# Second to fourth token block transposed by VectorE strips and a trip through DRAM instead of by TensorE

## The chip, the cores and the metric

The kernel runs on one core of a Trainium2 chip. The metric is the device time of one execution in microseconds (us); lower is better. The core has a matrix engine (TensorE, PE in the profile), VectorE (DVE), ScalarE (ACT), GpSimd (POOL) and SyncE (SP), which issues most of the transfers. All tensors are float32.

## What is computed

One layer on 2048 tokens of width 448: a layer norm, then attention with a compressive memory and a gated feed-forward network side by side, both added to the input. The reference, cut:

```
xn = layernorm(x)                                  # 2048 x 448
q, k, v = xn @ wq, xn @ wk, xn @ wv                # 16 heads of 28
for s in range(4):                                 # blocks of 512 tokens
    p = softmax(q_s k_s^T * scale + causal mask)
    a_mem = phi(q_s) M / (phi(q_s) z)              # memory of the earlier blocks
    o_s = g * a_mem + (1 - g) * p v_s
    M += phi(k_s)^T v_s;  z += sum phi(k_s)
A = o @ wo
B = (sigmoid(xn @ w_gate) * (xn @ w_up)) @ w_down  # 448 -> 1792 -> 448
out = x + A + B
```

## The kernel before

The program has a front (four blocks of 512 tokens, one after the other) and a long later part, in which the feed-forward network, the attention and the output projection share the engines.

A block of the front needs the normalised tokens with the 448 features on the partitions: `xs[b]`, a tile of 128 x 7 x 512. The features are in chunks of 128, 128, 128 and 64; the first 64 are kept twice in chunk 3. Each product is made in three parts, high by high, high by low and low by high, so `xs[b][:, 0:4]` holds the values rounded to the matrix engine's type and `xs[b][:, 4:7]` (and rows 64 to 127 of chunk 3) the differences to the full value. `TERMS` lists the eleven matmuls of a product: chunk 0 high by high, high by low, low by high, and so on.

In block b the order on TensorE is: four times `values` (11 matmuls into `pv`, one group of 128 tokens each; with a read of the memory, `recall`, behind some of them from the third block on), then seven times `keys_queries` (11 matmuls into `pp`, one chunk of 128 key or query features, k counts them), with `key_rows` (four transposes into `pk`) behind k = 2 to 5 and `update` (64 small matmuls into `pmm`) behind k = 6. Between them stands the preparation of block b+1: `statistics`, `rstd`, and for each of four token groups `normalise` (VectorE, L346) and `turn`, which is four TensorE transposes into a bank `pt` (L103), one ScalarE copy to the high part (L105) and two VectorE differences for the low part (L110, L111). `keys_queries` has ScalarE copy the product (L382), for keys and late queries two more passes there (L386, L387), a VectorE difference (L388), a store to DRAM (`qd`, L389) and a VectorE pass for `e` (L391).

On TensorE, ScalarE and VectorE the instructions of the front stand in the order in which the code writes them; the queues of SP and GpSimd are ordered by a scheduler. Each SP transfer also waits until the transfer eight before it has landed. `acc[b]` (128 x 4 x 448) holds the input of block b: the norm reads it, and later the products of both branches are added to it (L183, L831). `x_block(b)` loads it with token t*128 + p on partition p.

Of the kernel before, what the change touches and what calls it, by code (L numbers as in the profile page):

```python
# [9 lines left out]
F32 = mybir.dt.float32  # L10
# [59 lines left out]
def kernel(  # L70
# [45 lines left out]
    def x_block(b):  # L116
        return x[b * L:(b + 1) * L, :].rearrange("(t p) d -> p t d", p=P)

    ps = ctx.enter_context(tc.tile_pool(name="psum", bufs=1, space=PSUM))

# [27 lines left out]
    fd = [dram.tile([D, L], F32, name=f"fd{b}") for b in range(NB)]  # L148
    vd = [dram.tile([P, NT, H * 32], F32, name=f"vd{b}") for b in range(NB)]
    od = [dram.tile([H * 32, L], F32, name=f"od{b}") for b in range(NB)]  # L150

# [22 lines left out]
    def gated():  # L174
# [21 lines left out]
        def load_down(f, tag="rawd"):  # L196
            raw_down[f] = (mid.tile([P, 1024], F32, name="raw", bufs=2)[:, :D] if tag == "raw" else
                           mid.tile([P, D], F32, name="rawd", bufs=1))
            nc.sync.dma_start(raw_down[f], w_ffn[f][:, 1024:])
# [24 lines left out]
        for f0 in range(0, NF, FG):  # L224
# [3 lines left out]
            if f0 == 0:  # L228
                ahead[0, 0] = lambda: (load_down(1, "raw"), ready_up(1))
                ahead[0, 2] = lambda: load_up(2)  # L230
                ahead[1, 3] = lambda: load_up(3)
# [70 lines left out]
    with tc.tile_pool(name="front", bufs=2) as sb, tc.manual_schedule(engines=FRONT):  # L302
# [41 lines left out]
        def normalise(b, t, mean, y):  # L344
            xn = sb.tile([P, 512], F32, name="xn")
            V.tensor_scalar(xn[:, :D].rearrange("p (m h c) -> p h m c", h=H, c=4),  # L346
                              acc[b][:, t, :].rearrange("p (h m c) -> p h m c", h=H, c=4), mean, y,
                              op0=ALU.subtract, op1=ALU.mult)
            if b == 0:
                A.activation(xn[:, D:], xn[:, 384:D], AF.Copy)  # L350
            else:
                G.tensor_copy(xn[:, D:], xn[:, 384:D])
            return xn

        def turn(b, t, xn):
            transpose_split(bank("pt", "s"), xn, xs[b], t)

# [15 lines left out]

        stored = {}

# [74 lines left out]
        for c in range(4, 6):  # L450
            raw_qk.append(two_k("wqk_raw"))
            nc.sync.dma_start(raw_qk[c], w_qk[c])
        nc.sync.dma_start(acc[1], x_block(1))
        raw_qk.append(four_k(F32, "wqk_raw")[:, 0, :])
# [77 lines left out]
        for b in range(NB):  # L532
            last = b == NB - 1
            phi, xn = {}, {}
            if b > 1:
# [16 lines left out]
            if st and b > 0:  # L552
                st = rstd(*st)
                for n in range(2):
                    xn[n] = normalise(b + 1, n, *st[n])
            e = {}
            for k, c in enumerate((3, 4, 5, 6, 0, 1, 2) if last else range(7)):
# [13 lines left out]
                if (b, k) in ((0, 3), (1, 0)):  # L571
                    with tc.issue_after(stored[b, c]):
                        nc.sync.dma_start(acc[b + 2], x_block(b + 2))
                if (b, k) in ((2, 1), (3, 0)):
                    with tc.issue_after(stored[b, c]):
                        next(ffn)
                if last:
                    if k > 0:
                        next(ffn)
                    if 2 <= k < 6:  # L580
                        phi[k - 2] = phi_queries(b, k - 2)
                    if k > 4:
                        begin[k - 5]()
                        recall(b, k - 5, phi[k - 5])
                    continue
                if 2 <= k < 6:
                    key_rows(k - 2, e[k - 2])
                if k == 6:
                    update(b)
                n = k - 1 if b == 0 else k + 1  # L590
                if 2 <= n < 6:
                    turn(b + 1, n - 2, xn[n - 2])
                if 0 <= n < 4 and n not in xn:
                    xn[n] = normalise(b + 1, n, *st[n])
                if b == 2 and k == 6:
# [295 lines left out]
```

## Time and profile before

| | us |
|---|---|
| median of 3 runs (lowest to highest) | 680.28 (679.64 to 680.9) |
| the profiled execution | 679.62 |
| its span | 677.8 |
| TensorE busy in the span | 671.3 |
| VectorE busy | 569.2 |
| ScalarE busy | 338.6 |
| GpSimd busy | 149.3 |

The span is the time from the first to the last instruction of the profiled execution; the rest of its time lies around it. Rows of the profile name the source line (L103), the engine, the operation, the tile that is written and those that are read, the count, the busy time and the mean length of one in ns. A chain row has its start, its length and the work. The clock granted to TensorE was 0.999 over the span.

### The profile page before, as it was taken

How to read it: one execution, taken by the hardware profiler on the slowest of the kernel's cores; microseconds unless marked ns; L12 is line 12 of the kernel's file. 1: busy time of each engine (PE TensorE's matmuls, PEld its weight loads, DVE VectorE, ACT ScalarE, POOL GpSimd, SP SyncE). 2: the span in 40 equal slices, each digit the busy share in tenths (PEclk: the TensorE clock that was granted, in tenths of full speed). 3: DMA queues.
4: the chain of work that ended last, by engine and by line, in shares of the span. 5: the costliest groups of instructions: out<-in, count | busy, mean ns of one | idle time of the engine just before them, and what ended most of it. 6: DMA issues, size and time to landing. Idle time of an engine off the chain costs nothing.

```text
span 677.8 us, 11106 instructions
## 1 busy us (share of the span) xinstructions
PE 671.3 (99%) x3882; PEld 558.9 (82%) x3882; DVE 569.2 (84%) x987; ACT 338.6 (50%) x563; POOL 149.3 (22%) x360
## 2 busy tenths in 40 slices
PE   8999999999999999999999999999999999999998
PEld 7888888778878788788877878788787887888897
DVE  6765786685889899989989889899998899999854
ACT  4847564434454555555545455465545554544320
POOL 4520111001222222132222213232122221321000
PEclk9999999999999999999999999999999999999999
DMA  7446676794423133232325432325342432423352
GB/s 271 175 165 248 214 266 219 291 312 125 113 71 101 58 103 101 54 115 88 70 59 130 103 82 57 102 57 129 81 106 57 98 78 70 107 78 79 84 172 102
DMA packets 46327, 84.59 MB, mean 125 GB/s; under 512 B 6552, under 2 KB 20928, under 8 KB 45760
## 3 DMA queue, kind: packets, MB, share of 16 engines
q1 hardware_dynamic: 42736, 76.26, 36.9%
q0 software_dynamic: 3392, 7.52, 5.0%
q8 instruction: 31, 0.51, 0.3%
q14 instruction: 24, 0.20, 0.1%
q10 hardware_dynamic: 144, 0.11, 0.0%
HBM read 51.05 MB, written 32.64 MB: 123 GB/s over the span
## 4 chain that ended last, share of the span: by engine, by line
PE 97%; DMA 1%; DVE 1%; SPq 0%; ACT 0%; issue 0%; DVEq 0%
PE pgu L255 42%; PE pd L181 20%; PE pp L381 10%; PE st L639 6%; PE pa L725 5%; PE po L824 5%; PE pv L361 5%; PE n L433 2%; DMA acc<-in_x 1%; PE pt L103 1%; PE pk L401 1%; PE pmm L412 1%; DVE stats L320 0%; DVE xn L346 0%; DVE xs L110 0%
## 5 line engine op out<-in xcount | busy, mean ns | idle before, releaser
L255 PE MATMUL pgu<-xs,wgu 128*128 128x512 f32 x1232 | 302.6, 393 | 0.0
L255 PEld LDWEIGHTS pgu<-xs,wgu 128*128 128x128 f32 x1232 | 228.9, 188 | 46.4 <-issue 2.0
L181 PE MATMUL pd<-wdn,hh 128*128 128x448 f32 x672 | 155.3, 366 | 0.0
L181 PEld LDWEIGHTS pd<-wdn,hh 128*128 128x128 f32 x672 | 122.7, 188 | 11.6 <-issue 0.8
L654 POOL TENSOR_SCALAR_AFFINE_SELECT w<-w 128x256 f32<-128x256 f32 (+1 forms) x160 | 76.1, 478 | 231.5 <-ACT w L643 162.5
L707 ACT ACTIVATE w<-w 128x1024 f32<-128x1024 f32 (+1 forms) x96 | 87.9, 915 | 57.9 <-DVE w L703 57.9
L643 ACT ACTIVATE w<-st 128x512 f32<-128x512 f32 x128 | 75.6, 592 | 62.3 <-PE st L639 57.8
L703 DVE TENSOR_TENSOR w<-w,mb 128x1024 f32<-128x1024 f32 (+1 forms) x96 | 100.6, 1055 | 0.8
L661 DVE TRANSPOSE_TENSOR_REDUCE mx<-w 128x32 f32<-128x1024 f32 x64 | 78.9, 1233 | 6.6 <-POOL w L654 6.5
L381 PE MATMUL pp<-xs,wqk 128*128 128x512 f32 x308 | 77.7, 401 | 0.0
L183 DVE TENSOR_TENSOR acc<-pd,acc 128x448 f32<-128x448 f32 x112 | 67.5, 602 | 6.3 <-PE pd L181 6.3
L278 ACT ACTIVATE hh<-sg 128x512 fp32r<-128x512 f32 x56 | 35.3, 631 | 67.1 <-DVE sg L272 42.8
L381 PEld LDWEIGHTS pp<-xs,wqk 128*128 128x128 f32 x308 | 56.8, 188 | 13.4 <-issue 2.4
L639 PE MATMUL st<-qk 84*128 84x128 f32 (+3 forms) x256 | 62.1, 314 | 0.1
L262 ACT ACTIVATE sg<-pgu 128x512 f32<-128x512 f32 x56 | 33.2, 593 | 50.3 <-PE pgu L255 50.3
L639 PEld LDWEIGHTS st<-qk 84*128 84x128 f32 x256 | 47.9, 189 | 9.0 <-issue 1.4
L272 DVE SCALAR_TENSOR_TENSOR sg<-sg,pgu 128x512 f32<-128x512 f32 x56 | 37.7, 673 | 10.9 <-PE pgu L255 10.9
L388 DVE TENSOR_TENSOR qk<-pp,qk 128x512 fp32r<-128x512 f32 x28 | 19.3, 688 | 27.5 <-ACT e L386 21.5
L689 DVE STREAM_TRANSPOSE mb<-top 128x1024 f32<-128x1024 f32 x32 | 39.5, 1235 | 3.3 <-POOL top L686 3.2
L361 PE MATMUL pv<-wv,xs 128*128 128x448 f32 x176 | 39.8, 377 | 0.2
L281 DVE SCALAR_TENSOR_TENSOR hh<-sg,hh 128x512 fp32r<-128x512 f32 x56 | 38.3, 684 | 0.9 <-DMA qk<-qd 0.7
L725 PE MATMUL pa<-w,vv 128*32 128x128 f32 (+3 forms) x512 | 37.8, 436 | 0.0
(98 smaller groups left out, 624.4 us busy)
## 6 DMA issues: line engine op xcount, KB each, us to landing
qk<-qd SPq DMA_DIRECT2D x192, 112.0 KB
qd<-qk SPq DMA_DIRECT2D x28, 512.0 KB
raw<-in_w_ffn SPq DMA_DIRECT2D x14, 512.0 KB
vd<-vst SPq DMA_DIRECT2D x4, 1024.0 KB
vv<-vd SPq DMA_DIRECT2D x16, 256.0 KB
od<-w POOLq DMA_DIRECT2D x16, 256.0 KB, 4.2
sums<-od SPq DMA_DIRECT2D x32, 128.0 KB
out<-acc SPq DMA_DIRECT2D x15, 224.0 KB
```

What stands on the lines that cost most here:

```text
L181: T.matmul(pd[:, :D], l, r, start=n == 0, stop=n == len(mms) - 1)
L183: V.tensor_add(acc[b][:, t, :], pd[:, :D], acc[b][:, t, :])
L255: T.matmul(dst, wgu[f][:, w, side * P:(side + 1) * P], xs[b][:, a, :], start=n == 0, stop=n == len(TERMS) - 1)
L361: T.matmul(pv[:, :D], xs[b][:, a, t * P:(t + 1) * P], wv[w], start=n == 0, stop=n == len(TERMS) - 1)
L381: T.matmul(pp, wqk[c][:, w, :], xs[b][:, a, :], start=n == 0, stop=n == len(TERMS) - 1)
L639: T.matmul(st[:, at:at + L - kb * P], self.qk[:KS, 1, h, kb * P:(kb + 1) * P], self.qk[:KS, 0, h, kb * P:], start=True, stop=True)
L643: A.activation(w, st, AF.Copy)
L654: G.affine_select(d, d, pattern=pattern, base=0, channel_multiplier=-1, compare_op=ALU.is_ge, fill=MASK)
L661: V.tensor_reduce(self.mx[:, 32 * h:32 * h + 32], w3[:, h, :2 * L].rearrange("p (b n) -> p b n", n=32), axis=mybir.AxisListType.X, op=ALU. ...
L703: V.tensor_sub(w, w, m)
L707: A.activation(w, w, AF.Exp, scale=SCALE)
L725: T.matmul(pa[32 * j:32 * j + 32, kb * P:], self.vv[:, kb, 32 * j:32 * j + 32], self.pairs[j // 2].block(j % 2, kb), start=kb == 0, stop=k ...
```

## The change

Block 0 is prepared as before. For blocks 1 to 3 the TensorE transposes, the bank `pt` and the copies behind it are gone. The block is loaded with four consecutive tokens on a partition (`x_rows`). After each `normalise`, VectorE transposes the group in blocks of 32 x 32 (`strips`) into a stage with token order restored; the stage is an `acc` tile of another block that is free by then. After the fourth group, `spread` stores the stage to a DRAM tile `xd` with four SP transfers of 32 partitions each, in runs of 512 bytes, and GpSimd's queue loads it with the features on the partitions: 384 of them straight into the place of the low part of `xs`, 64 into a tile `tail`. At the end of the block `split_strips` makes the high part (two ScalarE copies) and the low part (two VectorE differences) for all 512 tokens at once. Normalising comes earlier: in the first block two groups behind k = 0 and two behind k = 1, later two ahead of k = 0 and one each behind k = 0 and k = 1. Since the stages overwrite `acc`, and tokens stand otherwise in it, blocks 1 to 3 are loaded a second time with `x_block` for the residual.

```diff
--- before.py
+++ after.py
@@ -116,6 +116,9 @@
     def x_block(b):
         return x[b * L:(b + 1) * L, :].rearrange("(t p) d -> p t d", p=P)
 
+    def x_rows(b):
+        return x[b * L:(b + 1) * L, :].rearrange("(p t) d -> p t d", t=NT)
+
     ps = ctx.enter_context(tc.tile_pool(name="psum", bufs=1, space=PSUM))
 
     banks = {"p": 2, "s": 2, "m": 1, "gu": 2, "pd": 1}
@@ -147,6 +150,7 @@
     qd = [dram.tile([2 * D, 2, L], F32, name=f"qd{b}") for b in range(NB)]
     fd = [dram.tile([D, L], F32, name=f"fd{b}") for b in range(NB)]
     vd = [dram.tile([P, NT, H * 32], F32, name=f"vd{b}") for b in range(NB)]
+    xd = [dram.tile([D, L], F32, name=f"xd{b}") for b in range(NB)]
     od = [dram.tile([H * 32, L], F32, name=f"od{b}") for b in range(NB)]
 
     mid = ctx.enter_context(tc.tile_pool(name="mid", bufs=3, reuse_waits="tile"))
@@ -227,6 +231,7 @@
             ahead = {}
             if f0 == 0:
                 ahead[0, 0] = lambda: (load_down(1, "raw"), ready_up(1))
+                ahead[0, 1] = lambda: nc.sync.dma_start(acc[3], x_block(3))
                 ahead[0, 2] = lambda: load_up(2)
                 ahead[1, 3] = lambda: load_up(3)
             if f0 + FG < NF:
@@ -349,11 +354,29 @@
             if b == 0:
                 A.activation(xn[:, D:], xn[:, 384:D], AF.Copy)
             else:
-                G.tensor_copy(xn[:, D:], xn[:, 384:D])
+                strips(b, t, xn)
             return xn
 
-        def turn(b, t, xn):
-            transpose_split(bank("pt", "s"), xn, xs[b], t)
+        def strips(b, t, xn):
+
+            s4 = stages[b].rearrange("p (i r t) -> p i r t", i=14, t=NT)
+            V.transpose(s4[:, :, :, t], xn[:, :D].rearrange("p (i r) -> p i r", r=32))
+
+        def spread(b):
+
+            for q in range(4):
+                nc.sync.dma_start(xd[b][:, q * P:(q + 1) * P].rearrange("(i c) n -> c i n", c=32),
+                                  stages[b][32 * q:32 * q + 32].rearrange("c (i n) -> c i n", n=P))
+            tail[b] = two_k("tail")
+            nc.gpsimd.dma_start(xs[b][:, 4:7, :].bitcast(F32), xd[b][:384].rearrange("(k p) n -> p k n", p=P))
+            nc.gpsimd.dma_start(tail[b][:64], xd[b][384:])
+
+        def split_strips(b):
+
+            A.activation(xs[b][:, 0:3, :], xs[b][:, 4:7, :].bitcast(F32), AF.Copy)
+            A.activation(xs[b][:64, 3, :], tail[b][:64], AF.Copy)
+            V.tensor_sub(xs[b][:, 4:7, :], xs[b][:, 4:7, :].bitcast(F32), xs[b][:, 0:3, :].bitcast(F32))
+            V.tensor_sub(xs[b][64:, 3, :], tail[b][:64], xs[b][:64, 3, :].bitcast(F32))
 
         def value_terms(b, t, pv, terms, n0=0, n1=len(TERMS)):
             for n in range(n0, n1):
@@ -371,7 +394,8 @@
             value_terms(b, t, pv, EARLY[1] if b == 0 else TERMS)
             store_values(b, t, pv)
 
-        stored = {}
+        stored, tail = {}, {}
+        stages = {b: acc[k].rearrange("p t d -> p (t d)") for b, k in ((1, 3), (2, 1), (3, 2))}
 
         def keys_queries(b, c):
 
@@ -450,7 +474,7 @@
         for c in range(4, 6):
             raw_qk.append(two_k("wqk_raw"))
             nc.sync.dma_start(raw_qk[c], w_qk[c])
-        nc.sync.dma_start(acc[1], x_block(1))
+        nc.sync.dma_start(acc[1], x_rows(1))
         raw_qk.append(four_k(F32, "wqk_raw")[:, 0, :])
         nc.sync.dma_start(raw_qk[6], w_qk[6])
         with nc.allow_non_contiguous_dma(reason="a strip's heads"):
@@ -531,7 +555,7 @@
         ffn = gated()
         for b in range(NB):
             last = b == NB - 1
-            phi, xn = {}, {}
+            phi = {}
             if b > 1:
                 phi = {i: phi_queries(b - 1, i) for i in range(NG)}
             st = None
@@ -552,7 +576,7 @@
             if st and b > 0:
                 st = rstd(*st)
                 for n in range(2):
-                    xn[n] = normalise(b + 1, n, *st[n])
+                    normalise(b + 1, n, *st[n])
             e = {}
             for k, c in enumerate((3, 4, 5, 6, 0, 1, 2) if last else range(7)):
                 e[c] = keys_queries(b, c)
@@ -570,11 +594,14 @@
                         V.tensor_scalar(gate_n, gate, -1.0, 1.0, op0=ALU.mult, op1=ALU.add)
                 if (b, k) in ((0, 3), (1, 0)):
                     with tc.issue_after(stored[b, c]):
-                        nc.sync.dma_start(acc[b + 2], x_block(b + 2))
+                        nc.sync.dma_start(acc[b + 2], x_rows(b + 2))
                 if (b, k) in ((2, 1), (3, 0)):
                     with tc.issue_after(stored[b, c]):
                         next(ffn)
                 if last:
+                    if k in (3, 5):
+                        b1 = k // 2
+                        nc.sync.dma_start(acc[b1], x_block(b1))
                     if k > 0:
                         next(ffn)
                     if 2 <= k < 6:
@@ -587,11 +614,13 @@
                     key_rows(k - 2, e[k - 2])
                 if k == 6:
                     update(b)
-                n = k - 1 if b == 0 else k + 1
-                if 2 <= n < 6:
-                    turn(b + 1, n - 2, xn[n - 2])
-                if 0 <= n < 4 and n not in xn:
-                    xn[n] = normalise(b + 1, n, *st[n])
+                for n in ((2 * k, 2 * k + 1) if b == 0 else (k + 2,)):
+                    if n < 4:
+                        normalise(b + 1, n, *st[n])
+                    if n == 3:
+                        spread(b + 1)
+                if k == 6:
+                    split_strips(b + 1)
                 if b == 2 and k == 6:
                     next(ffn)
             if last:
```

How this moves instructions, at three places. In the rows below the line numbers are those of each program (L346 is L351 after the change, L388 and L391 are L412 and L415, L389 is L413), and numbers behind names tell buffers apart.

VectorE in block 0, from the second key chunk on, before:

```order
55 L388 TENSOR_TENSOR qk<-pp,qk 128x512
56 L391 SCALAR_TENSOR_TENSOR e<-pp,e 128x512
57 L346 TENSOR_SCALAR xn<-acc_70,mv_329,y_340 128x16x7x4
58 L388 TENSOR_TENSOR qk<-pp,qk 128x512
59 L391 SCALAR_TENSOR_TENSOR e<-pp,e 128x512
60 L346 TENSOR_SCALAR xn<-acc_70,mv_329,y_340 128x16x7x4
```

and after:

```order
55 L351 TENSOR_SCALAR xn<-acc_70,mv_333,y_344 128x16x7x4
56 L363 STREAM_TRANSPOSE acc_72<-xn 128x448
57 L351 TENSOR_SCALAR xn<-acc_70,mv_333,y_344 128x16x7x4
58 L363 STREAM_TRANSPOSE acc_72<-xn 128x448
59 L412 TENSOR_TENSOR qk<-pp,qk 128x512
60 L415 SCALAR_TENSOR_TENSOR e<-pp,e 128x512
61 L351 TENSOR_SCALAR xn<-acc_70,mv_333,y_344 128x16x7x4
62 L363 STREAM_TRANSPOSE acc_72<-xn 128x448
63 L351 TENSOR_SCALAR xn<-acc_70,mv_333,y_344 128x16x7x4
64 L363 STREAM_TRANSPOSE acc_72<-xn 128x448
```

All four groups are normalised and turned around the second chunk's rows, where one group stood behind each chunk.

VectorE at the end of block 0 (`dense` is the memory that `update` leaves), before:

```order
70 L388 TENSOR_TENSOR qk<-pp,qk 128x512
71 L110 TENSOR_TENSOR xs_66<-pt,xs_66 128x3x128
72 L111 TENSOR_TENSOR xs_66<-pt,xs_66 64x128
73 L388 TENSOR_TENSOR qk<-pp,qk 128x512
74 L419 COPY dense_124<-pmm 28x128 x4
75 L110 TENSOR_TENSOR xs_66<-pt,xs_66 128x3x128
76 L111 TENSOR_TENSOR xs_66<-pt,xs_66 64x128
```

and after:

```order
67 L412 TENSOR_TENSOR qk<-pp,qk 128x512
68 L415 SCALAR_TENSOR_TENSOR e<-pp,e 128x512
69 L412 TENSOR_TENSOR qk<-pp,qk 128x512 x3
70 L443 COPY dense_128<-pmm 28x128 x4
71 L378 TENSOR_TENSOR xs_66<-xs_66 128x1536
72 L379 TENSOR_TENSOR xs_66<-tail,xs_66 64x512
```

The low part of the whole next block is made in one piece, behind the four `dense` rows, where before a quarter of it stood there.

GpSimd's queue around the first two hand-overs, after the change (before, 12 copies of 128 x 64 stood there, and no load):

```order
19 L493 TENSOR_TENSOR wqk_124<-wqk_raw,wqk_124 128x512
20 L371 DMA xs_66<-xd_92 128x3x512
21 L372 DMA tail<-xd_92 64x512
22 L446 DMA mst_126<-dense_128 28x4x32 x4
23 L371 DMA xs_67<-xd_93 128x3x512
24 L372 DMA tail<-xd_93 64x512
```

The load of the turned block stands behind the last weight split and ahead of the memory's transfers. On SP the four stores of a block stand behind the `qd` store of k = 1; the second loads of `acc` stand among the memory-query loads at the end of the second and third block.

## The prediction

> **What bounds the kernel now.** I read the page's busy rows and the shares of the chain that ended last, then that chain in order of time over the front, then single engines there.
>
> ```profile
> span 677.8 us, 11106 instructions
> PE 671.3 (99%) x3882; PEld 558.9 (82%) x3882; DVE 569.2 (84%) x987; ACT 338.6 (50%) x563; POOL 149.3 (22%) x360
> PE 97%; DMA 1%; DVE 1%; SPq 0%; ACT 0%; issue 0%; DVEq 0%
> ```
>
> TensorE is the bound: 97% of the chain is its own work. Nothing behind the front can absorb a delay, so each microsecond that TensorE stands still in the front lengthens the run by one, and each that is taken off it shortens it by one. The chain around the change from one block of tokens to the next (start, length, work):
>
> ```profile
> 30.35 0.44 PE pk L401 x4
> 30.78 0.44 PE pt L103 x4
> 31.22 2.54 PE pp L381 x11
> ...
> 40.59 1.22 PE pmm L412 x82
> 41.80 0.59 PE pt L103 x4
> 42.39 8.81 PE pv L361 x44
> 51.20 4.99 PE pp L381 x22
> ...
> 72.33 1.22 PE pmm L412 x82
> 73.54 4.61 PE pv L361 x22
> ...
> 88.52 2.52 PE pp L381 x11
> ...
> 107.18 1.22 PE pmm L412 x82
> 108.39 4.61 PE pv L361 x22
> ```
>
> TensorE passes from the memory sums (pmm) to the values of the next block (pv) without a gap, at 42.39, 73.54 and 108.39. The last quarter of the transposes (pt) even stands at 41.80: the values of token group 0 need only group 0, which was split long before.
>
> **What is removed.** Twelve groups of four transposes (pt, L103): eleven at 0.44 and one at 0.59, 5.4 us of TensorE, all on the chain. That is the whole possible gain. ScalarE loses 12 copies (L105) and VectorE 12 pairs of differences (L110, L111); neither was the bound.
>
> **What is added, and where it ends.** TensorE's first value matmul of block b+1 now waits for all 512 tokens: four strips on VectorE, a store to DRAM in four DMAs, a load by GpSimd's queue, one ScalarE copy of 1536 columns, one VectorE difference of 1536. I follow this chain in the clock of the old run. Prices of the compute steps:
>
> ```profile
> L346 DVE TENSOR_SCALAR xn<-acc,mv,y 128x448 f32<-128x448 f32 x16 | 8.5, 544 | 0.6
> L436 DVE STREAM_TRANSPOSE tb<-ts 128x512 f32<-128x512 f32 x12 | 8.5, 711 | 0.4
> L391 DVE SCALAR_TENSOR_TENSOR e<-pp,e 128x512 f32<-128x512 f32 x22 | 15.1, 688 | 0.0
> L93 ACT ACTIVATE wgu<-raw 128x1024 fp32r<-128x1024 f32 x14 | 14.8, 1056 | 0.0
> L93 ACT ACTIVATE wdn<-rawd 128x448 fp32r<-128x448 f32 x13 | 7.4, 570 | 0.1
> L94 DVE TENSOR_TENSOR wgu<-raw,wgu 128x1024 fp32r<-128x1024 f32 x14 | 16.9, 1210 | 4.0 <-ACT wgu L93 4.0
> L94 DVE TENSOR_TENSOR wdn<-rawd,wdn 128x448 fp32r<-128x448 f32 x13 | 8.2, 634 | 0.2
> ```
>
> A strip is a transpose of 448 columns: 711 x 448/512 = 0.62 us. Its output has a stride of 16 bytes, which no row shows on a transpose; bounds are 0.62 and twice that, and I take 0.62, since the normalisation (L346) also writes in permuted groups and costs no more per column. Normalise and strip are 1.16. From 448 to 1024 columns ScalarE takes 0.49 more and VectorE 0.58, so 1536 columns take 1.056 + 0.43 = 1.5 us and 1.21 + 0.51 = 1.7 us. Where VectorE stands in the three blocks:
>
> ```profile
> 27.61 0.17 DVE L570 TENSOR_SCALAR gate_n<-gate 128x4 f32<-128x4 f32 x1
> ...
> 58.01 0.69 DVE L391 SCALAR_TENSOR_TENSOR e<-pp,e 128x512 f32<-128x512 f32 x1
> ...
> 93.84 0.67 DVE L391 SCALAR_TENSOR_TENSOR e<-pp,e 128x512 f32<-128x512 f32 x1
> ```
>
> First hand-over: after 27.78 come two normalise-strip pairs, the 0.69 + 0.69 of key chunk 1, two pairs: 33.8. (This also holds up TensorE: the key rows of chunks 1 and 2 get their input at 31.5 and 35.2 rather than before 30.35 and 33.76. With four pt less it still reaches the end of pmm at about 42.4.) Second: chunk 1 ends at 58.7, one pair more: 59.9. Third: chunk 1 ends at 94.5, but two strips and a pair (1.24 + 1.16) have come in ahead and one pair follows: 98.1.
>
> The trip through DRAM: the trace has no such store, so its nearest rows are GpSimd's stores of 256 KB, the loads of vv in 512-byte runs and the qd store in 4 KB runs (columns of the last two end with the DMA share and GB/s).
>
> ```profile
> od<-tb POOLq DMA_DIRECT2D x12, 256.0 KB, 4.5
> DMA to landing us min/median/max: 2.3/4.5/6.4
> 258.90:260.30 1.40, 1.40 (x8) 1.13 (x6) 1.33 (x5) 0.00 (x0) 0.16 (x1) 1.00 0.93 207
> 26.00:27.00 1.00, 1.00 (x7) 0.81 (x6) 0.93 (x3) 0.97 (x3) 0.72 (x1) 1.00 1.00 410
> ```
>
> Spread: four DMAs, 917 KB in all in 512-byte runs. The fixed part is the shortest landing, 2.3; the data at 207 GB/s is 4.4, at 410 GB/s 2.2. I take 207, the row with the same run length: 6.7 us. The load of 786 KB in 2 KB runs: 4.5 for the first 256 KB, then 524 KB at 410 GB/s (1.3), or at half of it while qd stores share the engines (2.6): 5.8 to 7.1, and I take 6.5. Together 13.2 us from the last strip. The tail's 64 rows land behind it and are copied behind the 1.5 us.
>
> [...]
>
> Landing of the load: 33.8 + 13.2 = 47.0; 59.9 + 13.2 = 73.1; 98.1 + 13.2 = 111.3. First matmul 1.5 later: 48.5, 74.6, 112.8. It and the second (0.2 each: 8.81 over 44) need only the high parts; the third needs the difference, 1.7 later: 50.2, 76.3, 114.5. So the row of values runs as if begun 0.4 before: 49.8, 75.9, 114.1, against 42.39, 73.54 and 108.39. That is **7.4 + 2.4 + 5.7 = 15.5 us lost, the 5.4 of pt already taken off**.
>
> Restart: TensorE stands about 6 us in the first and third hand-over and 3 in the second. The only restart from a long stop that the trace has is the program's beginning:
>
> ```profile
> 1.78 3.85 PE L474 MATMUL warm<-ident 128*128 128x128 f32 x20 [1.78 <-POOL ident masks.py:199]
> 6.50 1.28 PE L477 MATMUL warm<-ident 128*128 128x128 f32 x10
> ```
>
> The same matmuls took 0.193 us a record in the first 3.85 us and 0.128 later, a loss of 3.85 x (1 - 0.128/0.193) = 1.3 us, after idle gaps of well under 1 us none. A stop of 6 us is nearer to the former, of 3 us undecided: I add 2 x 1.3 = **2.6** (bounds 0 and 3.9). [...]
>
> The profiled run took 679.62, its span 677.8. 677.8 + 15.5 + 2.6 = 695.9 of span, 697.7 for such a run; the median is 0.66 above the profiled run: **698.4 us**.
>
> **Costs put at nothing.** The second loads of the residual (3 x 896 KB, 2.2 us each at 410 GB/s) stand on SP ahead of the last block's value store, while the first addition that uses a residual of blocks 1 to 3 comes after those of block 0, which begin at 160.8; without that cover a VectorE addition would wait 2.2. They delay memory-query loads behind them by as much, which the later start of the values covers. SP's qd stores queue behind the spread; a buffer of qk is reused four chunks later. VectorE gets about 14.6 us and loses 10.2, and ScalarE is about even; both have idle time in the front.
>
> ```profile
> L183 DVE TENSOR_TENSOR acc<-pd,acc x112: 577/608/625, 160.8 to 652.5; 128x448 f32<-128x448 f32 x112
> ```
>
> **Rivals.** (1) The trip is hidden and only the split is late. ScalarE's 1536 columns stand behind the exponential of chunk 6, and VectorE's difference behind the four additions to the memory, which themselves wait for pmm:
>
> ```profile
> 73.48 0.63 ACT L387 ACTIVATE e<-e 128x512 f32<-128x512 f32 x1
> 74.75 1.23 DVE L421 TENSOR_TENSOR dense<-pmm,dense 28x128 f32<-28x128 f32 x4
> ```
>
> With 1.75 us of pt gone these end at 72.4 and 74.2; the difference ends at 75.9, and values run as from 75.5: +2.0 in the second and third, about +2.6 in the first, where pmm ends at 42.4: 6.6 us, 687. It holds if landing takes under 11 us from the strips; the chunk order speaks for it in the second block only. (2) The spread runs at 410 GB/s: 2.2 less in the first and third, 0.4 in the second, 4.8 in all: 693.6, and 691 if no restart cost is left. (3) The spread is slower than any row, since each DMA reads 32 partitions only: at half the rate 4.4 more in each block, 13.2: 711.6. For it speaks that no row has so many short runs from so few partitions; against it only that the vv row, with the same runs on 128 partitions, already pays for their length. (4) On the other side: the trip and both splits end before pmm does, and the 5.4 us remain, 675. It needs the split to begin 3.2 us ahead of pmm's end, and the order puts it behind chunk 6 on both engines: it decides only if the third matmul does not wait for the low part. The same mechanism half done would be no change.
>
> **How the numbers follow.** Forecast, trip late in all three blocks at 207 GB/s: 0.52, own range 694 to 703. Rival 1: 0.15. Rival 2: 0.18. Rival 3: 0.11. Rival 4 in full: 0.02, half done: 0.02. The time is 698.4; the range 688 to 712 leaves out rival 4, a part of 1 and a part of 3. What this measurement can tell from no change is about 0.2%, 1.4 us: faster 0.02, same 0.02, slower 0.96.
>
> **What would show it.** Chain: three stretches of "DMA xs<-xd", ScalarE and VectorE ahead of the value matmuls, 6, 3 and 6 us idle on TensorE; spread to landing 6.7, load 6.5; strips at 0.62, splits at 1.5 and 1.7; value matmuls at twice the length just after the stops; nothing new behind the front. Wrong would be: no idle time ahead of the values (rival 4), idle time released by VectorE alone (rival 1), or new waits in the later part, on the residuals.

## The result, and the profile after

| | before | after |
|---|---|---|
| median, us (lowest to highest) | 679.64 (679.38 to 680.9) | 717.69 (715.81 to 719.17) |
| the profiled execution, us | 679.62 | 717.48 |
| its span, us | 677.8 | 715.7 |
| clock granted to TensorE over the span | 0.999 | 0.971 |

The change makes the kernel slower: ratio 1.0554, 95% interval 1.0535 to 1.0573, 38 us. The direction was as predicted; the time is 19 us above the forecast of 698.4 and 6 us above the range's upper end.

The page after: its span, busy rows, the clock in 40 slices, and the group of the value matmuls, which the page before had as the last line (busy us, mean ns, idle time ahead):

```profile
span 715.7 us, 11012 instructions
PE 678.0 (95%) x3834; PEld 562.0 (79%) x3834; DVE 577.4 (81%) x981; ACT 339.3 (47%) x557; POOL 150.2 (21%) x354
PEclk9977979889999999999999999999999999999999
L384 PE MATMUL pv<-wv,xs 128*128 128x448 f32 x176 | 48.3, 431 | 27.4 <-ACT xs L376 25.0
...
L361 PE MATMUL pv<-wv,xs 128*128 128x448 f32 x176 | 39.8, 377 | 0.2
```

TensorE has 48 instructions fewer and yet 6.7 us more of busy time, and all that is odd about it lies in the first quarter of the span, where the clock row has its sevens and eights. The value matmuls (L384, L361 before) hold the loss: 27.4 us idle ahead of them instead of 0.2, and 48.3 us of work instead of 39.8.

The chain after, in order of time, around the three hand-overs (start, length, work):

```profile
35.15 1.00 DVE acc L363
...
37.85 5.14 DMA xd<-acc
43.63 11.21 DMA xs<-xd
54.87 1.49 ACT xs L376
56.39 1.77 DVE xs L378
58.20 11.06 PE pv L384 x42
...
79.78 6.29 DMA xd<-acc
86.64 9.10 DMA xs<-xd
...
99.09 6.70 PE pv L384 x20
...
129.26 4.31 DMA xd<-acc
134.21 7.57 DMA xs<-xd
...
145.13 5.92 PE pv L384 x20
```

Three times the path leaves TensorE and goes strip (L363), spread (`xd<-acc`), load (`xs<-xd`), split on ScalarE (L376), split on VectorE (L378), and back. The rest of the program only stands later: the additions to the residual begin at 198.9 instead of 160.8 and end at 690.2 instead of 652.5, 38.1 and 37.7 later, so they lost nothing on the way:

```profile
L187 DVE TENSOR_TENSOR acc<-pd,acc x112: 577/609/626, 198.9 to 690.2; 128x448 f32<-128x448 f32 x112
```

TensorE in order of time (the bracket holds the idle time ahead of the row and its releaser), and stretches of 10 us in which those values run (the number behind the five engines is the granted clock, then the DMA share and GB/s):

```profile
33.47 1.12 PE L425 MATMUL pk<-ident,e 128*128 128x128 f32 x4 [3.24 <-DVE e L415]
34.23 5.04 PE L405 MATMUL pp<-xs,wqk 128*128 128x512 f32 x11
...
56.41 1.11 PE L384 MATMUL pv<-wv,xs 128*128 128x448 f32 x2 [9.82 <-ACT xs L376]
```

```profile
50.00:60.00 10.00, 2.91 (x7) 2.12 (x8) 3.51 (x5) 2.01 (x2) 0.00 (x0) 0.50 0.45 179
60.00:70.00 10.00, 10.00 (x43) 9.09 (x42) 5.41 (x15) 5.16 (x8) 0.00 (x0) 0.83 0.01 2
```

After the stop the 42 remaining matmuls of block 1's values take 11.06 us, where 42 of the 44 took 8.4 before: the granted clock is 0.50 for the first 5 us, to 63, and 1.00 from 64 on. That is the restart, 2.6 us here. Transfers are not in its way: the DMA share is 0.01 in the second stretch. The same sum over the rows of 20 matmuls (4.0 us at full speed) gives 2.7 and 1.9 for the second and third.

From the chain the difference of the spans can be put together. As in the prediction, the values count as begun 0.4 ahead of the third matmul: 57.8, 98.7 and 144.7, against 42.39, 73.54 and 108.39. So the first hand-over loses 15.4. From the first to the second are 40.9 us instead of 31.15: 9.75, of which 2.6 are the first restart and 7.1 the second stop. From the second to the third are 46.0 instead of 34.85: 11.2, which is 2.7 of restart and 8.5 of stop. With the last restart, 1.9, the three restarts are 7.2, and the sum is 15.4 + 7.1 + 8.5 + 7.2 = 38.2; the spans differ by 37.9.

### The profile page after: what moved, and what is told of

Same layout as the page of the kernel before. It is cut to its first block, busy times and chain, and to the rows that moved or that the text cites. A ratio compares the mean times of both kernels' runs of the same rounds, so it can differ in the third digit from the quotient of the medians.

```text
span 715.7 us, 11012 instructions
## 1 busy us (share of the span) xinstructions
PE 678.0 (95%) x3834; PEld 562.0 (79%) x3834; DVE 577.4 (81%) x981; ACT 339.3 (47%) x557; POOL 150.2 (21%) x354
## 3 DMA queue, kind: packets, MB, share of 16 engines
q1 hardware_dynamic: 48736, 81.76, 38.1%
## 4 chain that ended last, share of the span: by engine, by line
PE 83%; DVE 7%; DMA 6%; ACT 1%; issue 1%; SPq 1%; DVEq 0%; POOLq 0%
PE pgu L260 40%; PE pd L185 19%; PE st L668 6%; PE pa L754 5%; PE po L853 5%; PE pv L384 5%; DMA xs<-xd 4%; PE pp L405 3%; DMA xd<-acc 2%; PE n L457 1%; DVE xn L351 1%; DVE acc L363 1%; DVE xs L378 1%; SPq L368 1%; DVE stats L325 1%
## 5 line engine op out<-in xcount | busy, mean ns | idle before, releaser
L732 DVE TENSOR_TENSOR w<-w,mb 128x1024 f32<-128x1024 f32 (+1 forms) x96 | 100.7, 1056 | 0.8
L405 PE MATMUL pp<-xs,wqk 128*128 128x512 f32 x308 | 79.4, 409 | 0.0
L384 PE MATMUL pv<-wv,xs 128*128 128x448 f32 x176 | 48.3, 431 | 27.4 <-ACT xs L376 25.0
L405 PEld LDWEIGHTS pp<-xs,wqk 128*128 128x128 f32 x308 | 58.5, 193 | 14.0 <-issue 2.4
L384 PEld LDWEIGHTS pv<-wv,xs 128*128 128x128 f32 x176 | 38.1, 223 | 35.4 <-ACT xs L376 25.3
L412 DVE TENSOR_TENSOR qk<-pp,qk 128x512 fp32r<-128x512 f32 x28 | 19.2, 685 | 33.9 <-ACT e L410 24.7
```

The source lines that it names most:

```text
L384: T.matmul(pv[:, :D], xs[b][:, a, t * P:(t + 1) * P], wv[w], start=n == 0, stop=n == len(TERMS) - 1)
L405: T.matmul(pp, wqk[c][:, w, :], xs[b][:, a, :], start=n == 0, stop=n == len(TERMS) - 1)
L732: V.tensor_sub(w, w, m)
```

## The experiments

Each version is compared with the kernel before on the same chip, whose median was 679.64 to 679.85. "Load" is the length of `xs<-xd` on the chain, in order of the hand-overs; the second figure of e10 is the `tail<-xd` issued behind it, which the chain shows there.

| kernel | median, us | ratio, 95% interval | load, us |
|---|---|---|---|
| after | 717.69 | 1.0535 to 1.0573 | 11.2, 9.1, 7.6 |
| e1: TensorE kept busy in the stops | 727.84 | 1.0687 to 1.0733 | off the chain |
| e5: the same, shorter | 716.22 | 1.0501 to 1.0564 | 12.3, 8.0, 9.4 |
| e3: load issued by ScalarE's queue | 718.59 | 1.0547 to 1.059 | 12.9, 7.7, 7.5 |
| e2: block 2's tokens loaded early | 716.06 | 1.0512 to 1.0549 | 9.5, 8.4, 8.1 |
| e9: e2 with smaller qd stores in block 0 | 712.08 | 1.046 to 1.0494 | 6.5, 7.4, 8.9 |
| e6: strips written without a stride | 716.77 | 1.0514 to 1.0567 | 9.3, 8.9, 9.4 |
| e7: load ahead of the stores on SP | 716.32 | 1.0508 to 1.0556 | off the chain |
| e4: block 1 by TensorE, as before | 701.57 | 1.0303 to 1.0344 | 9.1, 9.0 (two) |
| e8: all remedies together | 700.16 | 1.0282 to 1.0317 | off the chain |
| e10: blocks 2 and 3 only, strips earlier | 691.2 | 1.0141 to 1.0175 | 10.0, 10.1 (two) |

Two questions stood after the result: why the load takes 7.6 to 11.2 us and not 6.5, and whether the slow matmuls behind the stops are the clock.

### Is it the clock? e1 and e5

Small matmuls of the identity, whose result nobody reads, are put ahead of the first values of each block; the counts are those of e1, and e5 has (0, 44, 27, 27) and 11.

```diff
+        def hold(n):
+            pw = bank("hold", "pd")
+            for _ in range(n):
+                T.matmul(pw[:, :P], ident, ident, start=True, stop=True)
+                if b > 0 and t == 0:
+                    hold((0, 96, 52, 52)[b])
+                if b == 0 and k == 3:
+                    hold(24)
```

> The changed kernel, with small matmuls on the identity placed on TensorE in its three stops (96, 52 and 52 of them) and 24 ahead of the key rows of chunk 1 in the first block, results unused. Theory A (the clock is halved after each stop and the value matmuls behind it pay): the 42 matmuls behind the first stop take 8.4 us instead of 11.06, the 20 behind each of the others 4.0 instead of 6.70 and 5.92; no granted clock below 0.95 outside the stops; 717.7 - 7.3 = 710.4 us. Theory B (they are slow because transfers load the same memory): nothing changes, 716 to 719 us.

> The changed kernel with the same filling of TensorE's stops, shorter: one of these matmuls took 0.226 us in the run before, so 44, 27 and 27 of them in the stops and 11 ahead of the key rows of chunk 1. Theory A (the restart runs at half the clock): the value matmuls behind the stops take 8.4, 4.0 and 4.0 us, 717.7 - 7.3 = 710.4 us, granted clock near 1. Theory B (slow for another reason): 716 to 719 us.

Measured: e1 727.84 us, e5 716.22. In e1 a fill took 0.226 us (21.64 over 96 fills, two records each), so the fills outlasted the stops and the time rose. As times both expectations missed: 710.4 was expected of each, and e5 lies in the range of its theory B. As a test of the clock e1 is clear. The chain of e1:

```profile
46.15 21.64 PE hold L506 x192
67.78 8.81 PE pv L384 x44
...
110.38 4.41 PE pv L384 x22
```

With no stop in front of them the values run at their old length at once, 8.81 for 44 and 4.41 for 22, and the granted clock is 1.000 over the span. In e5 the fills end before the data is there in the first and third stop. TensorE and stretches of 2 us of it:

```profile
57.77 0.68 PE L384 MATMUL pv<-wv,xs 128*128 128x448 f32 x2 [2.74 <-ACT xs L376]
59.57 11.52 PE L384 MATMUL pv<-wv,xs 128*128 128x448 f32 x42 [1.12 <-DVE xs L378]
```

```profile
58.00:60.00 2.00, 0.88 (x3) 0.51 (x3) 1.97 (x2) 0.24 (x1) 0.00 (x0) 0.72 0.00 0
60.00:62.00 2.00, 2.00 (x7) 1.74 (x7) 1.90 (x6) 0.00 (x0) 0.00 (x0) 0.50 0.00 0
...
66.00:68.00 2.00, 2.00 (x12) 1.87 (x11) 1.90 (x4) 0.54 (x1) 0.00 (x0) 1.00 0.00 0
```

Idle for 2.74 us, two matmuls, idle for another 1.12: the clock falls to 0.50 and is back at 1.00 some 6 us later, and the 42 matmuls take 11.52. Behind the second hand-over of the same kernel, where the fills lasted nearly to the data, 20 of them took 4.28, nearly the full rate; behind the third, after 3.01 us idle, 5.59. So e5 lost two of its three restarts again. The restart is the clock: shown. How long an idle time it takes is bounded only: 2.74 and 1.12 with two matmuls between were enough here.

### What holds the load up? e3, e2 and e9

While the load runs, the DMA engines are not waiting for it alone. The queues of the kernel after between 43 and 55 us (packets, MB, share of 16 engines), and the issues on SP's queue ahead of it and in it:

```profile
DMA packets 1058, 3.90 MB, mean 325 GB/s; under 512 B 170, under 2 KB 217, under 8 KB 1056
q1 hardware_dynamic: 698, 2.91, 70.8%
q0 software_dynamic: 358, 0.97, 20.3%
```

```profile
36.16 2.77 SPq L368 DMA_DIRECT2D xd<-acc  x4
39.03 2.52 SPq L413 DMA_DIRECT2D qd<-qk  x2
41.61 0.82 SPq L597 DMA_DIRECT2D acc<-in_x  x1
42.52 4.56 SPq L413 DMA_DIRECT2D qd<-qk  x3
```

The load, with the tail, is 0.9 of the 3.9 MB that move. The other three quarters, on SP's queue q1, are of the five qd stores (512 KB each) and block 2's tokens (0.9 MB), which stood behind the spread on SP and are let go just ahead of the load and beside it. The order in time is plainer than the sum (share of the engines' time in stretches of 1 us, q1 with the stores and q0 with the load; the load is issued at 43.63 after the change and at 43.17 in e9, which is described below):

| from, us | 44 | 45 | 46 | 47 | 48 | 49 | 50 | 51 | 52 |
|---|---|---|---|---|---|---|---|---|---|
| after, q1, % | 94.3 | 100.7 | 75.4 | 88.6 | 96.0 | 61.4 | 48.2 | 49.3 | 51.0 |
| after, q0, % | 0 | 0 | 0 | 0 | 4.0 | 36.3 | 47.5 | 56.7 | 49.3 |
| e9, q1, % | 24.5 | 0 | 0 | 1.2 | 59.3 | 3.0 | 0 | 0 | 0 |
| e9, q0, % | 16.3 | 44.6 | 95.8 | 95.3 | 34.2 | 6.2 | 0.5 | 0 | 0 |

After the change no packet of the load moves in its first 4.4 us; then the two queues have about half of the engines each. Among the transfers that SP issued just ahead of the load are two qd stores and block 2's tokens, 1.97 MB; that the load waits for them is argued from this order. In e9, with the engines partly idle, the bulk of the load also comes only from 46 us on, 2.8 behind its issue, so not all of the 4.4 is due to the stores.

The rival is that the load is slow by itself: a GpSimd-issued transfer of this form. e3 has ScalarE's queue issue it, behind chunk 5:

```diff
-            nc.gpsimd.dma_start(xs[b][:, 4:7, :].bitcast(F32), xd[b][:384].rearrange("(k p) n -> p k n", p=P))
+            nc.scalar.dma_start(xs[b][:, 4:7, :].bitcast(F32), xd[b][:384].rearrange("(k p) n -> p k n", p=P))
```

> The changed kernel, with the load of the turned block issued by ScalarE's queue, behind its passes for chunk 5, instead of GpSimd's. Theory A (competition on the engines): issue to landing stays at 8 to 11 us in the first two blocks, 715 to 719 us. Theory B (GpSimd's queue is slow by itself): landing in about 4.5 us (2.3 fixed, 0.79 MB at 410 GB/s and the tail), stops shorter by 6, 3 and 3 us, about 706 us.

Measured 718.59 us, loads of 12.9, 7.7 and 7.5. The queue that issues it is not the reason.

e2 takes the 0.9 MB away: block 2's tokens are loaded right after the first loads of the program.

```diff
+        nc.sync.dma_start(acc[2], x_rows(2))
-                if (b, k) in ((0, 3), (1, 0)):
+                if (b, k) == (1, 0):
```

> The changed kernel, with block 2's tokens loaded right after the front's first loads instead of behind the fourth qd store. Theory A (the load xs<-xd is slow because qd stores and this 0.9 MB load share its engines): the first load lands in about 9 us instead of 11.2, the other two stay at 9.1 and 7.6; 717.7 - 2.2 = 715.5 us. Theory B (GpSimd's queue is slow by itself): first load 11.2, 717.7 us.

Measured 716.06 us, first load 9.45. The direction fits, but it decides little: the interval overlaps that of the kernel after, and the first load of the versions that keep these 0.9 MB in place lies anywhere from 9.3 (e6) to 12.9 (e3).

e9 goes on from e2 and shrinks the stores themselves. Of chunks 2 to 6 of block 0 only a quarter of the columns is stored; the other three quarters of those rows are filled early from a weight tensor, so the kernel leaves part of block 0's queries and keys out of the computation.

```diff
-            stored[b, c] = nc.sync.dma_start(qd[b][c * P:(c + 1) * P], qk.bitcast(F32)).ins
+            part = slice(0, P if 1 < c and b == 0 else L)
+            stored[b, c] = nc.sync.dma_start(qd[b][c * P:(c + 1) * P, :, part], qk[:, :, part].bitcast(F32)).ins
```

> The kernel with block 2's tokens loaded early, and in block 0 the qd stores of chunks 2 to 6 cut to a quarter of their columns; the other three quarters are filled from a weight tensor in the idle time of the queue at the start, so part of the keys and queries of block 0 is left out of the computation and the first hand-over has 0.66 MB beside the trip instead of 2.6 MB. Theory A (the load waits for its share of the engines): the first load lands in about 6 us instead of 9.45, the other two stay near 8.4 and 8.1; 716.1 - 3.5 = 712.6 us. Theory B (the load takes 8 to 11 us by itself): first load 9 us or more, 716 us.

Measured 712.08 us, 4.0 less than e2. Its chain, and the queues between 42 and 50 us:

```profile
43.17 6.49 DMA xs<-xd
...
80.26 7.38 DMA xs<-xd
...
125.68 8.88 DMA xs<-xd
```

```profile
q0 software_dynamic: 379, 0.97, 36.5%
q1 hardware_dynamic: 1144, 0.55, 25.9%
```

The same load, issued at the same time by the same queue, takes 6.49 us when 0.55 MB run beside it (in 8 us) instead of 2.91 (in 12), below every first load of the other kernels, while the two later loads, whose stores are whole, stay at 7.4 and 8.9. What the first load lost, it lost to the stores ahead of it and beside it. For the second and third this is inferred from the first, since their stores were not cut; after the change their first packets come in the third and the second us behind the issue (89 to 90 and 135 to 136), so they wait less and share more.

### The strip's stride: e6

The tokens are loaded so that the four strips stand side by side and a strip writes runs of 32 instead of single elements 16 bytes apart.

```diff
-            s4 = stages[b].rearrange("p (i r t) -> p i r t", i=14, t=NT)
-            V.transpose(s4[:, :, :, t], xn[:, :D].rearrange("p (i r) -> p i r", r=32))
+            s4 = stages[b].rearrange("p (i t r) -> p i t r", i=14, t=NT)
+            V.transpose(s4[:, :, t, :], xn[:, :D].rearrange("p (i r) -> p i r", r=32))
```

> The changed kernel, with the block's tokens laid on the partitions so that a strip writes runs of 32 elements instead of single elements 16 bytes apart (four loads of 32 partitions per block; the store to DRAM is the same). Theory A (the stride makes a strip cost 0.99 us rather than 0.62): strips of 0.62 us, strips done 1.5, 0.7 and 1.5 us earlier in the three blocks, 717.7 - 3.7 = 714.0 us. Theory B (a transpose whose output lies in blocks costs 0.99 us whatever the stride): strips of 0.99, 717.7 us.

A strip of each, grouped after, and in the first block of e6:

```profile
L363 DVE STREAM_TRANSPOSE acc<-xn 128x448 f32<-128x448 f32 x12 | 11.8, 984 | 0.4
```

```profile
L367 DVE STREAM_TRANSPOSE acc<-xn x4: 645/645/646, 30.7 to 36.2; 128x448 f32<-128x448 f32 x4
```

The stride is the whole difference, 0.98 against 0.65. The time, 716.77, is not told apart from that of the kernel after. In the first block the strips were not done earlier, but at 36.85 instead of 36.15: block 1's tokens, now loaded by four transfers, landed later, and the statistics began at 19.69 instead of 18.12. The three loads sum to 27.5 us where those of the kernel after sum to 27.9, only otherwise divided, and the third took 9.4 instead of 7.6.

### The load put first: e7

On SP the load is issued right behind the spread, and the qd and fd stores of that block behind the load.

```diff
-            nc.gpsimd.dma_start(xs[b][:, 4:7, :].bitcast(F32), xd[b][:384].rearrange("(k p) n -> p k n", p=P))
+            ahead_of[b] = nc.sync.dma_start(xs[b][:, 4:7, :].bitcast(F32),
+                                            xd[b][:384].rearrange("(k p) n -> p k n", p=P)).ins
...
+            if b + 1 in ahead_of:
+                with tc.issue_after(ahead_of[b + 1]):
+                    stored[b, c] = nc.sync.dma_start(qd[b][c * P:(c + 1) * P], qk.bitcast(F32)).ins
```

> The changed kernel, with the load of the turned block on SP's queue directly behind its four stores, and the qd and fd stores of the later chunks of that block held behind it (in the third hand-over one residual load of 0.9 MB also stands ahead of it). Theory A (the load is slow only because those stores run beside it): issue to landing about 4.5, 4.5 and 6.7 us instead of 11.2, 9.1 and 7.6, 717.7 - 12.2 = 705.5 us. Theory B (the load takes this long by itself, 2 KB runs out of a tile just written): 8 us or more each, 715 to 720 us.

Measured 716.32 us, 1.4 less instead of 12 (3.3 less in the profiled executions). The chain ahead of the first hand-over shows what came in the load's place:

```profile
37.77 4.17 DMA xd<-acc
...
43.18 6.03 DMA qd<-qk
...
49.62 0.60 ACT qk L408
50.22 1.37 ACT xs L378
```

The load is gone from the chain; a qd store is there. ScalarE's copy of chunk 6 (L408) needs the qk buffer of chunk 2, whose store now leaves only behind the load, and the split stands behind that copy on ScalarE. Against the kernel after, the third value matmul stands 4.3 us earlier in block 1, 6.7 in block 2 and 4.2 in block 3, where a second load of a residual stood ahead of the load on SP: the first two hand-overs gained 4.3 and 2.4, the third lost 2.5. When the load itself landed is not shown, since it shares its queue with the stores. Whichever goes first, the other is late: from 47 to 50 us the DMA engines are full (a share of 1.03 to 1.06, 422 to 430 GB/s).

### How much is each block worth? e4, e8 and e10

e4 leaves block 1 to TensorE as before (`turn` and the bank `pt` for b = 1), blocks 2 and 3 as changed.

```diff
-                for n in ((2 * k, 2 * k + 1) if b == 0 else (k + 2,)):
...
+                if b == 0:
+                    n = k - 1
+                    if 2 <= n < 6:
+                        turn(1, n - 2, x1[n - 2])
+                    if 0 <= n < 4:
+                        x1[n] = normalise(1, n, *st[n])
```

> The changed kernel, with block 1 prepared by TensorE as before and blocks 2 and 3 as changed. Theory A (each hand-over costs by itself and the costs add): the first stop with its slow restart goes, 717.7 - 15.4 - 2.6 = 699.7 us, the other two stops stay at 7 to 8 us. Theory B (the later stops are short only because the first one gave transfers time): the second and third get longer, 703 to 710 us.

Measured 701.57 us: 16.1 less, where the sum over the chain gave block 1 a share of 15.4 + 2.6 = 18.0. The two loads left are 9.07 and 8.95, the third 1.4 longer than after, which accounts for most of the rest. The time is nearer theory A's 699.7 than theory B's 703 to 710.

e8 puts all remedies together, for all three blocks: block 2's tokens early, strips without a stride, strips of blocks 2 and 3 ahead of their key chunks, the load first on SP, the split in quarters and, for blocks 2 and 3, behind chunk 5.

```diff
+                    if b > 0:
+                        st = rstd(*st)
+                        for n in range(NT):
+                            normalise(b + 1, n, *st[n])
+                        spread(b + 1)
...
+                if b > 0 and k == 5:
                     split_strips(b + 1)
```

> All remedies at once: plain strips; strips two chunks earlier in the first block and ahead of the key chunks in the others; the load ahead of the stores; block 2's tokens loaded early; the split in four parts, behind chunk 5 in the second and third block. Theory A (every stop is the trip arriving late, and nothing else was added to the path): the second and third stop vanish and the first is under 2 us, the 5.4 us of transposes remain as a gain in part: 675 to 682 us. Theory B (the added VectorE work and transfers cost time of their own once the trip is hidden): 683 to 700 us.

Measured 700.16 us. That is just past the upper end of theory B's range; theory A missed. Its chain at the first hand-over has the same store as that of e7 (`qd<-qk`, from 40.34, 6.98 long), then ScalarE's copy for the qk buffer, and then 42 value matmuls in 11.40 us from 50.84. TensorE still stands for 7 us there, where theory A had under 2, and restarts slowly: the same 42 took 11.06 after the change, with the granted clock at 0.50 for the first 5 us. The split stands behind that copy on ScalarE, so the store that was held back ends the wait. The second and third stops nearly go, but waits come up that the kernel before did not have: on VectorE's `e`, on the qk buffers, and for the fd loads of the memory queries.

e10 takes block 1 back to TensorE and gives blocks 2 and 3 their strips ahead of the key chunks, with the split in quarters behind chunk 5 and nothing held back on SP.

> Block 1 prepared by TensorE as before; blocks 2 and 3 by strips and the trip, but with all four strips ahead of the key chunks, so that the trip runs while the queue is nearly idle, and the split in four parts behind chunk 5. No store is held back. Theory A (only the late arrival costs): both stops vanish, eight groups of transposes (3.5 us) are gained: 679.8 - 3.5 = 676.3, at most 679 us. Theory B (once the trip is hidden, the added VectorE work and transfers cost their own time): 681 to 690 us.

Measured 691.2 us, the best of the versions with strips and still 11.4 slower than before, just above theory B's range. TensorE in order of time, at the two hand-overs and the waits near them, then two stretches of e10 and the same two of the kernel before:

```profile
73.78 2.67 PE L396 MATMUL pv<-wv,xs 128*128 128x448 f32 x11 [1.10 <-ACT xs L387]
...
82.19 1.10 PE L469 MATMUL n<-phi,mst 112*128 112x512 f32 x2 [1.60 <-DVE stats L329]
...
117.56 2.48 PE L396 MATMUL pv<-wv,xs 128*128 128x448 f32 x11 [1.61 <-DVE e L427]
122.51 1.83 PE L469 MATMUL n<-phi,mst 112*128 112x512 f32 x2 [2.46 <-DMA phi<-fd]
```

```profile
60.00:90.00 30.00, 25.44 (x237) 19.72 (x236) 20.45 (x45) 17.14 (x32) 3.71 (x6) 1.00 0.88 289
90.00:130.00 40.00, 34.60 (x270) 26.62 (x269) 26.10 (x49) 18.49 (x34) 6.48 (x11) 0.96 0.86 298
...
60.00:90.00 30.00, 30.00 (x264) 24.44 (x263) 23.52 (x53) 17.73 (x32) 5.10 (x11) 1.00 0.66 240
90.00:130.00 40.00, 40.00 (x313) 32.88 (x312) 30.21 (x58) 21.21 (x39) 5.62 (x11) 1.00 0.66 239
```

The values' first matmul now waits 1.1 us in the second hand-over and nothing in the third, and yet TensorE is idle for 4.6 + 5.4 = 10.0 us in these 70, where the kernel before has no idle time. The waits are short and have three kinds of releasers: ScalarE's split (`xs`); VectorE, which has strips or splits in front of what TensorE needs (`e`); and transfers that arrive late (`phi<-fd`), with the DMA engines at 0.86 to 0.88 instead of 0.66. The wait put down to `stats` is of the last kind: by the code that matmul needs `phi` and `mst` and no statistics, and the four transfers of `mst` are issued only from 78.54, since the `dense` rows stand behind the splits on VectorE. So hiding the trip did not make the strips free. How the remaining 10 us divide between VectorE's added work and the added traffic (917 KB out and in for a block, and the second load of its residual) was not separated.

## Why the prediction was wrong in size

By its own steps, the excess over the forecast at each hand-over (15.4, 7.1 and 8.5 us against 7.4, 2.4 and 5.7, so 8.0, 4.7 and 2.8), put on the steps by the times of the chain:

| step | predicted, us | measured, us | excess in the three hand-overs, us |
|---|---|---|---|
| strips done, counted from the values before | 33.8 in the first | 36.15 | 2.4, 0.4, 0.7 |
| spread, first issue to landing | 6.7 | 6.8, 7.7, 6.9 | 0.1, 1.0, 0.2 |
| load, from there to its landing | 6.5 | 11.9, 9.7, 8.2 | 5.4, 3.2, 1.7 |
| splits, to the third matmul | 3.2 | 3.4, 3.4, 3.4 | 0.2, 0.2, 0.2 |
| restart | 1.3, 0, 1.3 | 2.6, 2.7, 1.9 | 1.3, 2.7, 0.6 |

(The load's row includes some 0.6 us from the spread's landing to the issue by GpSimd; the excess of the strips is without the restart before them.)

**What held.** The path is the one described: trip late in all three hand-overs, ScalarE and VectorE one behind the other in front of the third matmul, slow matmuls after it, nothing new in the later part. The spread went by 207 GB/s and not by 410: in e7, where SP kept the qd stores back, it moved 198 to 233 GB/s from 37 to 41 us with the DMA share at 0.93 to 0.97. That the whole spread took 6.8, 7.7 and 6.9 us against 6.7 is in part luck: in e7 it took 5.9 in the first block (first issue 36.08, landing 41.94), so what is not data was nearer 1.5 us than the 2.3 of the forecast, and the qd stores that SP lets go beside its end, which the forecast left out, came on top. The splits took 1.49 and 1.77 against 1.5 and 1.7.

**The step that failed: the load.** "The load of 786 KB in 2 KB runs: ... 5.8 to 7.1, and I take 6.5". Its upper bound let the qd stores take half of the engines for the last 524 KB. Half is what they had in the first hand-over once the load moved; what the bound left out is the time before: 4.4 us passed without a packet of the load, where the bound has its first 256 KB landed after 4.5. Over the whole load q1 moved three quarters of the bytes. The reason lies in another step, "Costs put at nothing": SP's qd stores were said to queue behind the spread, and the only price looked for was the reuse of a qk buffer. But stores held back are stores that run later, and here they ran just ahead of the load and beside it: the first load took 6.5 us from its issue when they are cut (e9), 9.3 to 12.9 when not. The row is 10.3 of the 20 us; of the 5.4 in the first hand-over e9 took 4.7 away; that the 3.2 and 1.7 of the other two have the same cause is inferred. The forecast of 6.5 was the price of a load that nearly has the engines to itself.

**Strips.** 0.62 was one of two bounds, 0.62 and 1.24; the row is 0.98, and the reason given for the lower one (normalisation writes in permuted groups and pays nothing) did not carry over to a transpose; e6 shows 0.65 without the stride. In the first block VectorE was late besides: two of the normalisations took 1.54 and 1.27 us instead of 0.5 (last section). The excess of this term is 3.5.

**Restart.** The term had 1.3 for two stops and none for the second, taken from the beginning of the program. The second stop was not 3 us but 7.4, since the load was longer, and it counted. Each cost 1.9 to 2.7, 7.2 together, outside the bounds of 0 to 3.9 for all, and e1 shows that the clock is all of it. After the three stops (9.82, 7.43 and 7.72 us idle) the granted clock was 0.50 until about 63, 104 and 148 us, and back at 1.00 from 64, 105 and 149 on. At the beginning of the program, where the 1.3 was taken, the trace of the kernel before has it at 1.00 (2 to 6 us): the 1.3 was an estimate from the length of those matmuls alone, no measure of a clock of 0.50, and too low. The excess of this term is 4.6.

**The rivals.** Rival 3 gave 711.6, nearest to the time, and for a reason that did not occur: the spread was not slow. Rivals 1, 2 and 4 needed a shorter trip than even the forecast's. No rival had the load itself late because of what stood behind the spread, and the range had no room for it.

**Also missed, at no cost here.** The key rows of chunk 1 were predicted late by about a microsecond, with the end of pmm still at 42.4. TensorE waited 3.24 us for them, restarted at a granted clock of 0.50 (33 to 39 us; 5.04 us for eleven matmuls that take 2.77), and pmm ended at 46.6. The first values came at 56.4, so it was covered; it would have been covered by the forecast's 48.5 too.

## What to carry to other kernels

Price a trip through DRAM in the queue it will meet: list what its stores hold back on their queue, because those transfers can run ahead of the load that follows and beside it, as here; giving the load precedence moved the wait here to the buffers whose stores were then late (e7). Count a stop of TensorE as long as these (7.4 to 9.8 us) twice, once as idle time and once for what the first matmuls lose, here 1.9 to 2.7 us at a granted clock of 0.50. On TensorE, which bounds this run, 5.4 us of work taken off was worth less than the waits that the new dependence brought, and the value of a part is best read from a version that changes only that part (e4: one block of three carried 16 of 38 us).

## What the runs showed of the hardware

- **The transposes here paid for the stride of their output.** The 32 x 32 transpose of 448 columns took 0.98 us with elements 16 bytes apart and 0.65 with runs of 32; the normalisation, written in permuted groups, took 0.43 to 0.52 us where nothing stood beside it.
- **Two normalisations beside GpSimd's work took 1.54 and 1.27 us, the two without it 0.48 and 0.43.** VectorE and GpSimd in the first block, after:

```profile
27.60 1.54 DVE L351 TENSOR_SCALAR xn<-acc,mv,y 128x448 f32<-128x448 f32 x1
...
33.33 0.48 DVE L351 TENSOR_SCALAR xn<-acc,mv,y 128x448 f32<-128x448 f32 x1
```

```profile
27.59 1.30 POOL L493 TENSOR_TENSOR wqk<-wqk_raw,wqk 128x512 fp32r<-128x512 f32 x1 [0.96 <-ACT wqk L492]
```

The first ends 0.25 us after the GpSimd instruction that began with it; a second one, 1.27 long, ended 0.25 us after the next of these (29.75 to 31.03); the third, without such a neighbour, takes 0.48. That GpSimd's work held the two up is read from these times. No run separated it.

- **A load waited for its first packet and then had its half.** With stores of another queue issued just ahead of it, the first load after the change moved nothing for 4.4 us; from 50 to 53 us its queue q0 had 47.5 to 56.7% of the engines' time and q1 48.2 to 51.0%. With small stores (e9) q0 had 95% from 46 to 48 us.
- **The spread, in runs of 512 bytes, went at half the rate of what followed it.** Alone on the engines in e7, it moved 198 to 233 GB/s with the DMA share at 0.93 to 0.97; the stores and loads behind it moved 422 to 430 GB/s at 1.03 to 1.06. After the change it moved 201 and 203 GB/s from 37 to 39 us at 0.89 and 0.96, and the stores and loads 381 to 434 GB/s from 48 to 53 us at 0.96 to 1.06.
